# Pooled attention and a three-way max FFN on one core: long-run loads, pooling by adds on GpSimd, paired q transposes, 128-token value tiles and 512-token FFN blocks

## Chip, cores, metric

One core of one Trainium2 chip. The metric is the time of one execution on the device in microseconds (us), the median of several. "Span" is the time from the first to the last instruction in a profiled execution, some 2 to 3 us less. Outputs are compared with the reference.

Names: PE is TensorE (PEld its weight loads), DVE VectorE, ACT ScalarE, POOL GpSimd, SP the sync engine, which here only issues transfers. L189 is line 189 of the kernel in question; a trailing `q` (SPq, POOLq) is an engine's sequencer, where transfers are issued.

## The reference

```python
# q, k, v: [8 batches, 8 heads, 576 tokens, 64], float32
k_p = k.reshape(B, H, 72, 8, D).mean(axis=3)          # pooled over 8 tokens
v_p = v.reshape(B, H, 72, 8, D).mean(axis=3)
attn = softmax(q @ k_p.T / sqrt(64))                  # 576 x 72 for each head
x = (attn @ v_p) as [4608 tokens, 512]                # heads side by side
h = max(x @ w1, x @ w2, x @ w3)                       # w: [512, 768]
out = h @ w_out                                       # [768, 512], float32
```

## The kernel before

Tokens are kept in their order. For each batch: q is transposed, k and v are pooled by matmuls with a 0/1 matrix, then scores, exp, values, transposes; the FFN of batch b-1 fills TensorE beside batch b's attention. The order of instructions on each engine is fixed when the kernel is built.

```python
# q: runs of 2 tokens (512 B); one transpose for each of 36 [128 tokens, 64] pieces
qsrc = q[b]....rearrange("(g p j) d -> p g j d", p=128, j=2)
nc.gpsimd.dma_start(out=qb_, in_=qsrc)
for u in range(n_t):
    nc.tensor.transpose(pqt[:, u, :], qb_[:, tidx // 2, tidx % 2, :], ident)

# k, v: five loads each, runs of one token (256 B), pooled by 2 x 5 matmuls of 512 columns
for c in range(5):
    nc.gpsimd.dma_start(out=kvt, in_=src[b, :, CHUNK0[c]:CHUNK0[c] + 128, :]
                        .rearrange("h s d -> s h d"))
for c in range(5):
    nc.tensor.matmul(p, ptr[:, c, :], kvts[c], start=(c == 0), stop=(c == 4))

# values: 48 matmuls a batch with 96-wide weights
nc.tensor.matmul(pavn[:, 3 * i + j, :], eTs[i][:, QC * j:QC * j + QC], vp8[:, h, :], ...)

# FFN, for each batch: two halves of 288 columns, and five output tiles (the fifth half used)
for i in range(2):
    for jc in range(6):
        for wi in range(3):
            for kc in range(4):
                nc.tensor.matmul(pw, w_sb[wi][:, kc, ...], xT[:, kc, ncol], ...)
for m in range(5):
    n0, r0 = (128 * m, 0) if m < 4 else (448, 64)
    ...
# ... (cut)
```

The softmax here doesn't subtract the row's maximum and nothing guards it: scores larger than these inputs give would overflow.

Of the kernel before, what the change touches and what calls it, by code (L numbers as in the profile page):

```python
# [14 lines left out]
def kernel(  # L15
# [23 lines left out]
    HALF = 288  # L39
    QC = 96  # L40
    NG = (H * S) // 256
    KCH = C // 128
    JCH = DFF // 128

    const = ctx.enter_context(tc.tile_pool(name="const", bufs=1))
    wtsp = ctx.enter_context(tc.tile_pool(name="wts", bufs=1))
    sb1 = ctx.enter_context(tc.tile_pool(name="sb1", bufs=1))
    sb2 = ctx.enter_context(tc.tile_pool(name="sb2", bufs=2))
    sb3 = ctx.enter_context(tc.tile_pool(name="sb3", bufs=3))
    kvsb = ctx.enter_context(tc.tile_pool(name="kvsb", bufs=12))  # L50
    psp = ctx.enter_context(tc.tile_pool(name="psp", bufs=1, space=bass.MemoryType.PSUM))

    def q_load(b):
        qb_ = sb1.tile([128, NG, 2, D], BF16, name="qb", tag="qb")
        qsrc = q[b].rearrange("h s d -> (h s) d").rearrange(
            "(g p j) d -> p g j d", p=128, j=2)
        nc.gpsimd.dma_start(out=qb_, in_=qsrc)  # L57
        return qb_

    qb0 = q_load(0)  # L60
# [6 lines left out]
    CHUNK0 = [0, 128, 256, 384, 448]  # L67
    ptf = const.tile([128, 5, 128], F32, name="ptf", tag="ptf")
    nc.gpsimd.memset(ptf, 0.0)
    for c in range(5):  # L70
        o = CHUNK0[c]
        pz = ptf[:, c, 0:Sp]
        nc.gpsimd.memset(pz, 1.0)
        nc.gpsimd.affine_select(out=pz, in_=pz, compare_op=ALU.is_ge, fill=0.0,
                                base=o, pattern=[[-8, Sp]], channel_multiplier=1)
        nc.gpsimd.affine_select(out=pz, in_=pz, compare_op=ALU.is_ge, fill=0.0,
                                base=7 - o, pattern=[[8, Sp]],
                                channel_multiplier=-1)
        if c == 4:
            nc.gpsimd.affine_select(out=pz, in_=pz, compare_op=ALU.is_ge,  # L80
                                    fill=0.0, base=-64, pattern=[[0, Sp]],
                                    channel_multiplier=1)
    ptr = const.tile([128, 5, 128], F16, name="ptr", tag="ptr")
    nc.scalar.copy(out=ptr, in_=ptf)
    bias8 = const.tile([128, 1], F32, name="bias8", tag="bias8")
    nc.gpsimd.memset(bias8, float(POOL))

    w_sb = [wtsp.tile([128, KCH, DFF], F16, name=f"mw{wi}", tag=f"mw{wi}")
            for wi in range(3)]
    wo_sb = wtsp.tile([128, JCH, C], F16, name="mwo", tag="mwo")  # L90

    def load_weights():
        for t, wap in zip(w_sb, (moe_w1, moe_w2, moe_w3)):
            nc.gpsimd.dma_start(out=t,
                                in_=wap.rearrange("(kc p) j -> p kc j", p=128))
        nc.gpsimd.dma_start(out=wo_sb,
                            in_=moe_w_out.rearrange("(jc p) c -> p jc c", p=128))

    def preproc_q(b, qb_):
        qT = sb2.tile([128, NG * 256], BF16, name="qT", tag="qT")  # L100
        nc.gpsimd.memset(qT[64:128, :], 0.0)  # L101
        qTv = qT[0:64].rearrange("d (g p j) -> d g j p", p=128, j=2)
        for grp in range(5):
            n_t = 8 if grp < 4 else 4
            pqt = psp.tile([64, 8, 128], BF16, name="pqt", tag="misc", bufs=2)
            for u in range(n_t):
                tidx = grp * 8 + u
                nc.tensor.transpose(pqt[:, u, :], qb_[:, tidx // 2, tidx % 2, :],  # L108
                                    ident)
            g0 = grp * 4  # L110
            nc.scalar.copy(out=qTv[:, g0:g0 + n_t // 2, :, :], in_=pqt[:, 0:n_t, :])  # L111
        return qT

    def pool_kv(b):
        ps = {}
        for name, src in (("k", k), ("v", v)):
            p = psp.tile([128, H * D], F32, name=f"p{name}8", tag="misc", bufs=2)
            kvts = []
            for c in range(5):
                kvt = kvsb.tile([128, H, D], F16, name=f"{name}c", tag="kv")  # L120
                nc.gpsimd.dma_start(  # L121
                    out=kvt,
                    in_=src[b, :, CHUNK0[c]:CHUNK0[c] + 128, :].rearrange(
                        "h s d -> s h d"))
                kvts.append(kvt)
            for c in range(5):
                nc.tensor.matmul(p, ptr[:, c, :], kvts[c],  # L127
                                 start=(c == 0), stop=(c == 4))
            ps[name] = p
        kp8 = sb2.tile([Sp, H, D], BF16, name="kp8", tag="kp8")  # L130
        nc.scalar.copy(out=kp8, in_=ps["k"][0:Sp].rearrange("sp (h d) -> sp h d", d=D))
        pkt = psp.tile([64, H, Sp], BF16, name="pkt", tag="misc", bufs=2)
        for h in range(H):
            nc.tensor.transpose(pkt[:, h, :], kp8[:, h, :], ident[0:Sp, 0:Sp])
        kpT = sb2.tile([128, H, Sp], BF16, name="kpT", tag="kpT")
        nc.gpsimd.memset(kpT[64:128, :, :], 0.0)
        nc.scalar.copy(out=kpT[0:64], in_=pkt)
        vp8 = sb2.tile([Sp, H, 65], F16, name="vp8", tag="vp8")
        nc.scalar.copy(out=vp8[:, :, 0:D],
                       in_=ps["v"][0:Sp].rearrange("sp (h d) -> sp h d", d=D))  # L140
        nc.scalar.activation(out=vp8[:, :, D:65], in_=ps["v"][0:Sp, 0:H],
                             func=FT.Identity, bias=bias8[0:Sp], scale=0.0)
        return kpT, vp8

    def heads(b, qT, kpT, vp8, xnat):
        for h in range(H):
            pavn = psp.tile([QC, 2 * 3, 65], F32, name="pavn", tag="att", bufs=3)
            eTs = []
            for i in range(2):
                col0 = S * h + HALF * i  # L150
                psc = psp.tile([Sp, HALF], F32, name="psc", tag="att", bufs=3)
                nc.tensor.matmul(psc, kpT[:, h, :], qT[:, col0:col0 + HALF],  # L152
                                 start=True, stop=True)
                eT = sb3.tile([Sp, HALF], F16, name="eT", tag="eT")
                nc.scalar.activation(out=eT, in_=psc, func=FT.Exp,  # L155
                                     scale=1.0 / 64.0)
                eTs.append(eT)
            for i in range(2):
                for j in range(3):
                    nc.tensor.matmul(pavn[:, 3 * i + j, :],  # L160
                                     eTs[i][:, QC * j:QC * j + QC],
                                     vp8[:, h, :], start=True, stop=True)
            rcp = sb2.tile([QC, 6], F32, name="rcp", tag="rcp")
            nc.vector.reciprocal(out=rcp, in_=pavn[:, :, 64])  # L164
            nc.vector.tensor_tensor(  # L165
                out=xnat[:, :, D * h:D * h + D], in0=pavn[:, :, 0:D],
                in1=rcp.to_broadcast([QC, 6, D]), op=ALU.mult)

    def xpose(b, xnat, xT):
        for cj in range(6):  # L170
            pxt = psp.tile([128, KCH, QC], F16, name="pxt", tag="misc", bufs=2)
            for kc in range(KCH):
                nc.tensor.transpose(pxt[:, kc, :],  # L173
                                    xnat[:, cj, 128 * kc:128 * kc + 128],
                                    identh[0:QC, 0:QC])
            nc.scalar.copy(out=xT[:, :, QC * cj:QC * cj + QC], in_=pxt)  # L176

    def moe(b, xT):
        hT = sb2.tile([128, JCH, S], F16, name="hT", tag="hT")
        for i in range(2):  # L180
            ncol = bass.ts(i, HALF)
            for jc in range(JCH):
                t1 = t2 = None
                for wi in range(3):
                    tag, nb = ("m1a", 2) if wi != 1 else ("m1b", 1)
                    pw = psp.tile([128, HALF], F32, name=f"pw{wi}", tag=tag,
                                  bufs=nb)
                    for kc in range(KCH):
                        nc.tensor.matmul(  # L189
                            pw, w_sb[wi][:, kc, bass.ts(jc, 128)],  # L190
                            xT[:, kc, ncol],
                            start=(kc == 0), stop=(kc == KCH - 1))
                    if wi == 0:
                        t1 = sb2.tile([128, HALF], F32, name="t1", tag="t1")
                        nc.vector.tensor_copy(out=t1, in_=pw)  # L195
                    elif wi == 1:
# [18 lines left out]
    for b in range(B):  # L215
        qT = preproc_q(b, qb0 if b == 0 else q_load(b))
        kpT, vp8 = pool_kv(b)
        if b == 0:
            load_weights()
# [38 lines left out]
```

## Time and profile before

| | before |
|---|---|
| time | 346.65 us (346.37 to 346.81, three runs); 342.7 to 347.8 in later calls |
| span of the profiled run | 343.5 us |
| TensorE busy | 90% |
| software queue's share of the 16 DMA engines | 67.8% |

The lines of this profile, and how they are read, are in the prediction.

### The profile page before, as it was taken

How to read it: one execution, taken by the hardware profiler on the slowest of the kernel's cores; microseconds unless marked ns; L12 is line 12 of the kernel's file. 1: busy time of each engine (PE TensorE's matmuls, PEld its weight loads, DVE VectorE, ACT ScalarE, POOL GpSimd, SP SyncE). 2: the span in 40 equal slices, each digit the busy share in tenths (PEclk: the TensorE clock that was granted, in tenths of full speed). 3: DMA queues.
4: the chain of work that ended last, by engine and by line, in shares of the span. 5: the costliest groups of instructions: out<-in, count | busy, mean ns of one | idle time of the engine just before them, and what ended most of it. 6: DMA issues, size and time to landing. Idle time of an engine off the chain costs nothing.

```text
span 343.5 us, 6436 instructions
## 1 busy us (share of the span) xinstructions
PE 309.8 (90%) x2528; PEld 203.4 (59%) x2528; DVE 165.9 (48%) x416; ACT 151.7 (44%) x290; POOL 122.9 (36%) x134
## 2 busy tenths in 40 slices
PE   0678589999999999999999999999999999999992
PEld 0425366665567566675567556765577466766750
DVE  0004226771387326771387226761487227764840
ACT  1634364435753275505753276406743286412012
POOL 8997259650744029500743028500800000000000
PEclk9999999999999999999999999999999999999999
DMA  7999999943890219903990229903990210003012
GB/s 69 68 153 209 186 127 117 110 31 124 89 148 2 90 52 159 66 0 131 91 140 0 94 52 159 62 1 138 97 96 0 103 37 2 2 14 125 0 41 101
DMA packets 109408, 28.22 MB, mean 82 GB/s; under 512 B 102464, under 2 KB 104768, under 8 KB 109376
## 3 DMA queue, kind: packets, MB, share of 16 engines
q0 software_dynamic: 104128, 18.36, 67.8%
q1 hardware_dynamic: 5248, 9.44, 7.6%
q8 instruction: 20, 0.33, 0.4%
q14 instruction: 12, 0.10, 0.1%
HBM read 36.70 MB, written 9.44 MB: 134 GB/s over the span
## 4 chain that ended last, share of the span: by engine, by line
PE 68%; ACT 15%; DMA 8%; POOL 6%; issue 3%; ACTq 0%; DVE 0%; POOLq 0%
PE pw L189 33%; PE po L207 14%; ACT qT L111 9%; PE pavn L160 7%; DMA qb<-in_q_dram 6%; ACT eT L155 4%; PE psc L152 3%; PE pqt L108 3%; PE pxt L173 3%; PE pk L127 2%; PE pv L127 2%; DMA out_dram<-osb 2%; POOL vc L121 1%; POOL kc L121 1%; POOL qT L101 1%
## 5 line engine op out<-in xcount | busy, mean ns | idle before, releaser
L189 PE MATMUL pw<-xT,mw 128*128 128x288 f16 x1152 | 180.0, 287 | 0.2
L189 PEld LDWEIGHTS <-mw 128*128 128x128 f16 x1152 | 106.2, 99 | 25.3 <-issue 0.6
L195 DVE COPY t<-pw 128x288 f32<-128x288 f32 x96 | 43.5, 453 | 64.0 <-PE pw L189 62.5
L155 ACT ACTIVATE eT<-psc 72x288 f16<-72x288 f32 x128 | 46.5, 402 | 40.9 <-PE psc L152 39.8
L210 ACT COPY osb<-po 128x512 f32<-128x512 f32 (+1 forms) x40 | 23.4, 584 | 93.0 <-PE po L207 76.4
L201 DVE TENSOR_TENSOR hT<-t,pw 128x288 f16<-128x288 f32 x96 | 42.9, 447 | 36.6 <-PE pw L189 31.3
L207 PE MATMUL po<-mwo,hT 128*128 128x512 f16 x240 | 53.3, 379 | 1.5 <-ACT osb L210 1.5
L198 DVE TENSOR_TENSOR t<-t,pw 128x288 f32<-128x288 f32 x96 | 43.3, 451 | 23.3 <-PE pw L189 17.2
L111 ACT COPY qT<-pqt 64x1024 bf16<-64x1024 bf16 (+1 forms) x40 | 43.9, 1184 | 19.6 <-PE pqt L108 19.0
L160 PEld LDWEIGHTS <-eT 72*96 72x96 f16 x384 | 31.4, 130 | 28.6 <-ACT eT L155 24.6
L160 PE MATMUL pavn<-vp,eT 72*96 72x65 f16 x384 | 40.0, 220 | 5.8 <-ACT eT L155 2.0
L57 POOL DMA_DIRECT2D qb<-in_q_dram x8 | 9.9, 1234 | 95.3 <-PE pqt L108 72.9
L207 PEld LDWEIGHTS <-hT 128*128 128x128 f16 x240 | 23.5, 98 | 28.5 <-issue 1.8
L121 POOL DMA_DIRECT2D vc<-in_v_dram x40 | 35.3, 918 | 9.9 <-DMA mwo<-in_moe_w_out_dram 2.9
L108 PE MATMUL pqt<-ident,qb 128*64 128x128 bf16 x288 | 25.1, 236 | 14.8 <-DMA qb<-in_q_dram 11.7
L101 POOL MEMSET qT<- 64x4608 bf16 x8 | 31.6, 3946 | 18.7 <-PE psc L152 18.6
L121 POOL DMA_DIRECT2D kc<-in_k_dram x40 | 35.2, 898 | 2.5 <-PE psc L152 1.9
L165 DVE TENSOR_TENSOR xnat<-pavn,rcp 96x384 f16<-96x384 f32 x64 | 35.1, 548 | 0.8
L108 PEld LDWEIGHTS <-qb 128*64 128x64 bf16 x288 | 21.1, 120 | 23.4 <-DMA qb<-in_q_dram 12.3
L152 PE MATMUL psc<-qT,kpT 128*72 128x288 bf16 x128 | 34.8, 308 | 0.0
L164 DVE RECIPROCAL rcp<-pavn 96x6 f32<-96x6 f32 x64 | 12.2, 190 | 40.8 <-PE pavn L160 40.5
L176 ACT COPY xT<-pxt 128x384 f16<-128x384 f16 x48 | 20.8, 479 | 17.4 <-PE pxt L173 16.9
(31 smaller groups left out, 119.6 us busy)
## 6 DMA issues: line engine op xcount, KB each, us to landing
out_dram<-osb SPq DMA_DIRECT2D x32, 256.0 KB, 2.0
kc<-in_k_dram POOLq DMA_DIRECT2D x40, 128.0 KB, 6.6
vc<-in_v_dram POOLq DMA_DIRECT2D x40, 128.0 KB, 6.9
qb<-in_q_dram POOLq DMA_DIRECT2D x8, 576.0 KB, 7.1
mw<-in_moe_w_dram POOLq DMA_DIRECT2D x3, 768.0 KB, 12.3
out_dram<-osb SPq DMA_DIRECT2D x8, 128.0 KB, 2.3
mwo<-in_moe_w_out_dram POOLq DMA_DIRECT2D x1, 768.0 KB, 18.3
```

Source lines behind the costliest of these rows:

```text
L108: nc.tensor.transpose(pqt[:, u, :], qb_[:, tidx // 2, tidx % 2, :], ident)
L111: nc.scalar.copy(out=qTv[:, g0:g0 + n_t // 2, :, :], in_=pqt[:, 0:n_t, :])
L121: nc.gpsimd.dma_start(out=kvt, in_=src[b, :, CHUNK0[c]:CHUNK0[c] + 128, :].rearrange("h s d -> s h d"))
L152: nc.tensor.matmul(psc, kpT[:, h, :], qT[:, col0:col0 + HALF], start=True, stop=True)
L155: nc.scalar.activation(out=eT, in_=psc, func=FT.Exp, scale=1.0 / 64.0)
L160: nc.tensor.matmul(pavn[:, 3 * i + j, :], eTs[i][:, QC * j:QC * j + QC], vp8[:, h, :], start=True, stop=True)
L165: nc.vector.tensor_tensor(out=xnat[:, :, D * h:D * h + D], in0=pavn[:, :, 0:D], in1=rcp.to_broadcast([QC, 6, D]), op=ALU.mult)
L189: nc.tensor.matmul(pw, w_sb[wi][:, kc, bass.ts(jc, 128)], xT[:, kc, ncol], start=(kc == 0), stop=(kc == KCH - 1))
L195: nc.vector.tensor_copy(out=t1, in_=pw)
L198: nc.vector.tensor_tensor(out=t2, in0=t1, in1=pw, op=ALU.max)
L201: nc.vector.tensor_tensor(out=hT[:, jc, ncol], in0=t2, in1=pw, op=ALU.max)
L207: nc.tensor.matmul(po, hT[:, jc, n0:n0 + 128], wo_sb[:, jc, :], start=(jc == 0), stop=(jc == JCH - 1))
```

## The change

The intent: less work for TensorE (pooling by adds on an idle engine, fewer and fuller transposes, no half-used output tile) and loads in long runs. To let two q tokens of a partition be transposed at once, tokens are reordered inside the kernel: column 32 t + r of a batch is token 18 r + t, and the stores put them back, 32 rows at a time.

```diff
-        qsrc = ... "(g p j) d -> p g j d", p=128, j=2          # runs of 512 B
+        kt <- k[b] "(p i j d) -> p i j d", p=96, i=6, j=8      # SP's queue, 12288 B runs
+        vt <- v[b] "h (sp j) d -> sp h j d", j=8               # SP's queue, 2048 B runs
+        qb <- q[b] "(g p t d) -> p g t d", g=2, p=128, t=18    # POOL's queue, 4608 B runs
+    (two buffers each)
-                nc.tensor.matmul(p, ptr[:, c, :], kvts[c], ...)        # pooling, 10 a batch
+        eng = nc.vector if b == 0 else nc.gpsimd
+            for n in (4, 2):
+                e.tensor_tensor(out=t[:, :, 0:n, :], in0=t[:, :, 0:n, :],
+                                in1=t[:, :, n:2 * n, :], op=ALU.add)
+            for o in outs:
+                e.tensor_tensor(out=o, in0=t[:, :, 0, :], in1=t[:, :, 1, :], op=ALU.add)
+        fold(eng, kt, [kp2[:, :, 0, :], kp2[:, :, 1, :]])
+        fold(nc.gpsimd, vt, [vp_all[:, b, :, 0:D]])
-                nc.tensor.transpose(pqt[:, u, :], qb_[:, tidx // 2, tidx % 2, :], ident)
+                nc.tensor.transpose(pqt[:, u, :], qb[:, g, 2 * i:2 * i + 2, :], ident)
-                    nc.tensor.matmul(pavn[...], eTs[i][:, QC * j:QC * j + QC], vp8[:, h, :], ...)
+        for n in ((128, 128, 128, 128, 64) if b % 2 == 0 else (64, 128, 128, 128, 128)):
+                nc.tensor.matmul(pav[0:n, ...], ets[h][:, c0:c0 + n], vp_all[:, b, h, :], ...)
-    def moe(b, xT):      # 2 x 288 columns, 5 output tiles
+    def moe(n):          # 512 columns across batches, 4 output tiles
+                if wi == 0: nc.scalar.copy(out=t, in_=pw)       # the first copy goes to ScalarE
+            for u in range(4):
+                nc.sync.dma_start(out=dst[:, g, :], in_=osb[32 * u:32 * u + 32, :])
 ... (cut; PSUM is now: scores 2 banks, values 2 banks, transposes 1 bank, FFN 3 banks)
```

The four weight loads are issued by POOL straight after batch 0's q. xT holds all 4608 tokens.

## The prediction

> **What bounds the kernel now.** I read the page first: which engine is full, at which clock, and what the path to the end runs through.
>
> ```profile
> PE 309.8 (90%) x2528; PEld 203.4 (59%) x2528; DVE 165.9 (48%) x416; ACT 151.7 (44%) x290; POOL 122.9 (36%) x134
> ...
> PE   0678589999999999999999999999999999999992
> ...
> PEclk9999999999999999999999999999999999999999
> DMA  7999999943890219903990229903990210003012
> ...
> PE 68%; ACT 15%; DMA 8%; POOL 6%; issue 3%; ACTq 0%; DVE 0%; POOLq 0%
> ```
>
> TensorE is busy 90% of 343.5 us at full clock, no other engine over half. The first five slices (8.6 us each) are its only thin ones. So the time is TensorE work, plus a start, plus what is lost between. The DMA engines are full at the start only. The groups give mean durations, but matmuls overlap (1152 of 287 ns would be 331 us, busy is 180), so I take the step from one start to the next in the timeline:
>
> ```profile
> 298.80 7.27 PE L189 MATMUL pw<-xT,mw 128*128 128x288 f16 x58
> ...
> 305.91 6.64 PE L207 MATMUL po<-mwo,hT 128*128 128x512 f16 x30
> ```
>
> 58 steps in 7.11 us: 122.6 ns for 288 columns. In the chain the 30 po matmuls take 6.47 us: 215.7 ns for 512. The same way, from one batch's TensorE timeline:
>
> ```profile
> 159.09 0.63 PE L108 MATMUL pqt<-ident,qb 128*64 128x128 bf16 x8
> 159.66 1.28 PE L189 MATMUL pw<-xT,mw 128*128 128x288 f16 x9
> ...
> 165.47 1.24 PE L127 MATMUL pk<-kc,ptr 128*128 128x512 f16 x5
> 166.55 1.24 PE L127 MATMUL pv<-vc,ptr 128*128 128x512 f16 x5
> ...
> 182.25 0.33 PE L173 MATMUL pxt<-identh,xnat 96*128 96x96 f16 x4 [0.15 <-ACT xT L176]
> 182.41 0.29 PE L189 MATMUL pw<-xT,mw 128*128 128x288 f16 x1
> ```
>
> q transposes step 71 ns (0.57/8), pooling matmuls 216 ns, output transposes 40 ns (0.16/4); from their neighbours, scores 125 ns, values about 48 ns, k transposes 47 ns. Work of one batch: 144 x 122.6 + 30 x 215.7 = 24.1 us of FFN; 36 x 71 + 10 x 216 + 8 x 47 + 16 x 125 + 48 x 48 + 24 x 40 = 10.4 us of attention. Eight batches: 276 us. The po blocks start 38.3 us apart in the chain, so 3.8 us per batch is lost to short waits, mostly 0.15 to 0.25 us before a matmul that needs a ScalarE result. The remaining 67.5 us of the span: about 34 us in the start (dense FFN from 46 us, about 12 us of work done by then), 27 us in seven periods, 6.5 us in the tail (two output buffers waiting for the store).
>
> The start is not one wait:
>
> ```profile
> 8.26 1.92 PE L108 MATMUL pqt<-ident,qb 128*64 128x128 bf16 x16 [8.26 <-DMA qb<-in_q_dram]
> ...
> 44.07 1.92 PE L108 MATMUL pqt<-ident,qb 128*64 128x128 bf16 x16 [3.48 <-DMA qb<-in_q_dram]
> ```
>
> q lands at 8.3 us; then ten k/v loads and the weights are issued one by one by POOL, batch 0's attention crawls head by head, and the second q, queued behind the weights, holds TensorE until 44 us.
>
> **What the Trainium skill says.** (1) "TensorE: Matmul & The Clock Gate", section "Wait — 56ns, not 53.3ns?": a warm stream steps N/2.4 GHz plus about 2.5 ns. The trace agrees: 122.6 for 288, 215.7 for 512. So a longer matmul saves only the 2.5 ns. (2) Same page, "Weight-path perf modes": the fast weight load needs exactly 128 weight columns. The trace fits: 128-wide pxt steps 40 ns, just its 96 columns; 64-wide pqt steps 71 where its 128 columns are 53. (3) "GPSIMD Engine Reference", section 3: a two-input fp32 add of 2048 elements takes 4497 ns, 2.2 ns an element, about twice VectorE. No trace here has one. (4) "DMA: Bandwidth & Descriptors", Specifications: line rate needs runs of 512 B or more. The page has 102464 of 109408 packets under 512 B and the software queue at 67.8%, which agrees, but TensorE hardly waits for DMA after 46 us.
>
> **The change, part by part, on TensorE.**
> - FFN blocks of 512 tokens: 9 blocks x (72 + 24) x 215.7 ns = 186.4 us, against 8 x 24.1 = 193. Gain 6.6 us: 5.2 of it from the fifth, half-wasted output tile of each batch, only 1.4 from longer matmuls.
> - Pooling on POOL: removes 10 x 216 ns, 2.16 us a batch, **17 us** in all. POOL's adds: k 1536+768+2x384 and v 2048+1024+512 elements a partition, 6656 x 2.2 ns = an estimate of 14.6 us a batch from (3). That is half of a period and runs ahead: hidden, except at the start.
> - Paired q transposes: 18 instead of 36, each 128-wide, estimated at 56 ns: 1.0 us against 2.56, gain **12 us**.
> - Values: 40 instead of 48, 128-wide weights except the last tile, about 40 ns: 1.66 against 2.3 us, gain 5 us. k transposes 6 x 40 ns; output transposes 16 x 56 + 4 x 30 ns = 1.0 us; scores stay at 2.0 us. All nearly nothing.
> Attention becomes 1.0 + 0.24 + 2.0 + 1.66 + 1.0 = 5.9 us a batch, 47 us in all. **TensorE work: 186.4 + 47.2 = 233.6 us, 42 us less.**
>
> Other engines, by the trace's slopes (ScalarE 384 columns 479 ns, 512 columns 585; VectorE 288 columns 450 ns, 384 columns 548): ScalarE gets the first FFN copy: 10 x 0.585 a block; per batch three q copies at 0.80, eight exps of 576 at 0.64, five xT copies at 0.585, 10.4 us. Sum 9 x 5.85 + 8 x 10.4 = 136 us. VectorE: 12 x 0.68 a block, 5.9 us a batch: 121 us. Neither becomes a bound.
>
> **What is lost around it.** Start: k and v go out by the sync queue, q and the weights by POOL at once. Weights and second q took about 18 us for 7.4 MB read in the old trace, so some 400 GB/s; k, v, q of batch 0, the weights and batch 1's loads are 13.4 MB, 34 us. q and k of batch 0 at about 9 us; q transposes in one PSUM buffer until 14.5; k transposes and two VectorE copies until 17; eight heads, one score buffer, 1.35 us each, until 28; v's adds on POOL end near 24; four value tiles at 1.9 us and the copy: FFN from about 37 us, up to 46 if TensorE's fixed order has the second q's transposes (landing near 35 us) ahead of the values. About 7 us of work is done by then: I choose a loss of **33 us**, hardly better than before. Steady: about 21 waits a batch (8 scores, 5 values, 5 output transposes, 4 others; before some 20 that cost anything) with single score, value and transpose buffers, but FFN matmuls to fill; I choose 3 us x 7 = **21 us**. Tail: four stores a tile at 0.33 us issue, 2 us landing, three output buffers: **5 us**. Span 233.6 + 33 + 21 + 5 = 292.6; the time is 3.1 us over the span now, so 296; since xT holds all tokens, attention can run ahead and the last two blocks or so should be free of waits, which I put at 4 us: **292 us**.
>
> **Rivals.**
> 1. *The single buffers become the bound* (two-bank scores, two-bank values, one transpose bank). The serial chain of a batch is about 8 x 1.2 + 5 x 1.9 + 3 x 1.5 + 2.5 = 26 us against 29 us of TensorE work per batch (233.6/8): close. For it: the order within each engine is fixed, and now the first FFN copy sits in ScalarE's line behind exps. Against it: FFN work depends on none of these buffers, and parts of successive batches overlap. It would give 310 to 320 us.
> 2. *The start gets worse or POOL's adds hold it*: POOL has q, four weights and v's adds in one queue, and the weights take half the bandwidth from k and v. For it: the old trace shows just such a wait for q. Against it: no ten loads one after another. Worth 10 us more: 302.
> 3. *Nearly all is packed*: waits below 1.5 us a batch, FFN from 33 us: 275 us.
> 4. *The transfers were the bound*: the long runs would then be the gain. TensorE's 90% and the DMA row's zeros in mid-kernel speak against it; I give this part nothing after the start.
>
> **Range and chances.** Work is known to within a few us, the start to 8 either way, steady loss to 10, a common cause (a poor order) only upwards: 276 to 312. For less than 2% gain (over 339.7 us) the 42 us would have to be lost almost wholly again, for which only rival 1 at its worst has room: faster 0.96, within 2% 0.03, slower 0.01.
>
> **What would show it.** Right: 864 FFN matmuls (1392 before), stepping 215.7 ns in dense stretches; pqt stepping near 56 ns, values near 40; no pk or pv; POOL adds near 2.2 ns an element with no long wait on them after batch 1; DMA packets down to a tenth; ScalarE near 136 and VectorE near 121 us busy; first pw between 33 and 46 us. Wrong: TensorE waits on exps, VectorE's normalisation or transposes of over 5 us a batch (rival 1), on POOL's adds or q in the first 60 us (rival 2), or small matmuls that do not step as narrow columns suggest, which would raise the 47 us.

## The result, and the profile after

| | time, median | runs | ratio to before, 95% interval |
|---|---|---|---|
| before | 346.51 us | 342.74 to 346.81 | |
| after | 307.96 us | 306.41 to 308.39 | 0.891, 0.886 to 0.896 |

A ratio is the mean time of one kernel's fast runs over the mean of the other's of the same rounds, so it is not quite the ratio of the two medians. The kernel before had medians of 346.5, 345.7, 345.2 and 345.6 us in the four calls, so times of different calls compare to about 1 us.

The page of the kernel after:

```profile
PE 257.3 (84%) x1664; PEld 130.4 (43%) x1664; DVE 127.8 (42%) x211; ACT 133.0 (43%) x219; POOL 124.6 (41%) x72
...
PE   0144470299999999999999999999999999999991
...
PEclk9999996579999999999999999999999999999998
DMA  7999999988644986982610450050022003104014
```

TensorE is less busy than before and the thin start is longer: eight slices of 7.7 us, the seventh empty. Behind it the row is full. The same in stretches (columns: busy us of each engine with the number of instructions, the granted TensorE clock, the DMA engines' busy share, GB/s):

```profile
0.00:41.25 41.25, 13.40 (x97) 9.04 (x97) 13.50 (x18) 11.19 (x16) 25.38 (x23) 1.00 0.99 234
41.25:45.20 3.95, 3.94 (x12) 1.07 (x11) 0.82 (x2) 0.86 (x2) 3.93 (x3) 1.00 1.05 263
45.20:59.58 14.38, 0.00 (x0) 0.00 (x0) 0.69 (x1) 0.00 (x0) 14.12 (x7) 0.61 0.96 227
59.58:258.73 199.15, 198.56 (x1365) 101.65 (x1366) 96.30 (x167) 108.71 (x180) 81.15 (x41) 0.99 0.43 99
```

The FFN begins at 41 us, does eight matmuls, and then TensorE stands still for 14.4 us with the DMA engines full. What it waits for, in the timeline and among the issues (columns: queue, count, KB each, median us from issue to landing):

```profile
18.97 4.49 POOL L98 TENSOR_TENSOR vt<-vt 72x2048 f32<-72x2048 f32 x1 [12.91 <-DMA vt<-in_v_dram]
...
23.41 0.74 POOL L64 DMA_DIRECT2D qb<-in_q_dram  x1
...
59.59 0.82 PE L114 MATMUL pqt<-ident,qb 128*128 128x128 bf16 x6 [14.40 <-DMA qb<-in_q_dram]
60.20 1.91 PE L179 MATMUL pw<-xT,mw 128*128 128x512 f16 x4
61.91 0.85 PE L114 MATMUL pqt<-ident,qb 128*128 128x128 bf16 x6
```

```profile
qb<-in_q_dram POOLq DMA_DIRECT2D x8, 576.0 KB, 8.6
mw<-in_moe_w_dram POOLq DMA_DIRECT2D x3, 768.0 KB, 27.5
mwo<-in_moe_w_out_dram POOLq DMA_DIRECT2D x1, 768.0 KB, 50.8
```

Batch 1's q is issued by POOL at 23.4 us, behind v's first add, and lands 36.1 us later; the last weight load, issued at 5.2 us, takes 50.8 us. Meanwhile SP has fetched k and v ahead: its issues are at 0.7, 1.2, 1.7, 2.1, 12.4, 31.1, 41.2, 45.5 and 52.7 us.

The wait has a second cost. The four FFN matmuls behind it take 1.71 us to the next start, 427 ns each instead of the 216 of later stretches; by the starts in the trace this lasts until 65.4 us. The granted clock of this stretch is 0.59 (third figure from the right):

```profile
59.58:66.70 7.12, 7.11 (x38) 4.06 (x39) 1.07 (x2) 2.98 (x4) 1.27 (x2) 0.59 0.80 197
```

Steps of 426 ns also follow the waits of 7.1 us in q1_first and 12.2 us in kv_single, and none follow one of 3.5 us in combined (216 ns).

The work itself steps as forecast. From the chain and the TensorE timeline of the kernel after:

```profile
258.73 15.54 PE pw L179 x72
274.27 5.18 PE po L196 x24
```

```profile
162.14 0.42 PE L151 MATMUL pav<-vp,et 72*128 72x65 f16 x8
162.40 1.89 PE L179 MATMUL pw<-xT,mw 128*128 128x512 f16 x8
...
172.55 0.50 PE L114 MATMUL pqt<-ident,qb 128*128 128x128 bf16 x6
172.89 1.03 PE L179 MATMUL pw<-xT,mw 128*128 128x512 f16 x4
```

15.54/72 and 5.18/24 are 215.8 ns; the paired transposes step 0.34/6 = 57 ns, the 128-wide values 0.26/8 = 33 ns. The account takes the forecast's steps for all three columns; with the steps as measured the work after is some 231 us, and the loss between some 17:

| us | before | predicted | after |
|---|---|---|---|
| TensorE's work | 276 | 233.6 | 233.6 |
| lost in the start | 34 | 33 | 52 (59.6 less 7.6 of work done) |
| lost between | 27 | 17 (21 less 4) | 14.5 (199.15 less 184.6) |
| lost at the end | 6.5 | 5 | 6.4 (300.2 to 306.6) |
| time over span | 3.1 | 3.1 | 1.8 |

### The profile page after: what moved, and what is told of

Read it like the earlier page. It is cut to its first block, busy times and chain, and to the rows that moved or that the text cites. A ratio compares the mean times of both kernels' runs of the same rounds, so it can differ in the third digit from the quotient of the medians.

```text
span 306.6 us, 4320 instructions
## 1 busy us (share of the span) xinstructions
PE 257.3 (84%) x1664; PEld 130.4 (43%) x1664; DVE 127.8 (42%) x211; ACT 133.0 (43%) x219; POOL 124.6 (41%) x72
## 2 busy tenths in 40 slices
DMA packets 17078, 36.47 MB, mean 119 GB/s; under 512 B 2720, under 2 KB 5024, under 8 KB 16288
## 3 DMA queue, kind: packets, MB, share of 16 engines
q1 hardware_dynamic: 12512, 28.32, 35.7%
## 4 chain that ended last, share of the span: by engine, by line
PE 78%; DMA 18%; POOL 1%; DVE 0%; ACT 0%; issue 0%; SPq 0%; ACTq 0%
PE pw L179 46%; PE po L196 15%; DMA qb<-in_q_dram 12%; DMA vt<-in_v_dram 6%; PE psc L135 5%; PE pav L151 4%; PE pqt L114 3%; PE pxt L164 3%; POOL vt L98 1%; PE pkt L120 1%; DVE t L187 0%; DVE xn L159 0%; ACT xT L168 0%; ACT osb L200 0%; SPq L58 0%
## 5 line engine op out<-in xcount | busy, mean ns | idle before, releaser
L179 PE MATMUL pw<-xT,mw 128*128 128x512 f16 x648 | 162.0, 386 | 0.1
L179 PEld LDWEIGHTS <-mw 128*128 128x128 f16 x648 | 57.8, 99 | 53.9 <-issue 2.5
L187 DVE TENSOR_TENSOR t<-t,pw 128x512 f16<-128x512 f16 x54 | 37.0, 686 | 88.9 <-PE pw L179 77.7
L98 POOL TENSOR_TENSOR vt<-vt 72x2048 f32<-72x2048 f32 (+1 forms) x16 | 54.8, 3425 | 16.1 <-DMA vt<-in_v_dram 15.6
L138 ACT ACTIVATE et<-psc 72x576 f16<-72x576 f32 x64 | 41.4, 646 | 34.1 <-PE psc L135 34.1
L190 DVE TENSOR_TENSOR hT<-t,pw 128x512 f16<-128x512 f16 x54 | 37.0, 685 | 29.9 <-PE pw L179 28.5
L184 ACT CAST t<-pw 128x512 f16<-128x512 f32 x54 | 31.6, 585 | 41.1 <-PE pw L179 40.4
L98 POOL TENSOR_TENSOR kt<-kt 96x1536 f32<-96x1536 f32 (+1 forms) x14 | 36.6, 2614 | 3.1 <-DMA kt<-in_k_dram 2.7
L135 PE MATMUL psc<-qT,kz 128*72 128x288 bf16 x128 | 29.5, 304 | 6.3 <-ACT et L138 5.1
L200 ACT COPY osb<-po 128x512 f32<-128x512 f32 x36 | 21.1, 587 | 16.7 <-PE po L196 15.1
L159 DVE TENSOR_TENSOR xn<-pav,rcp 128x512 f16<-128x512 f32 (+1 forms) x40 | 27.5, 687 | 1.0
L114 PEld LDWEIGHTS <-qb 128*128 128x128 bf16 x144 | 11.4, 109 | 38.3 <-DMA qb<-in_q_dram 29.5
L64 POOL DMA_DIRECT2D qb<-in_q_dram x8 | 6.0, 752 | 33.7 <-PE pqt L114 32.9
## 6 DMA issues: line engine op xcount, KB each, us to landing
kt<-in_k_dram SPq DMA_DIRECT2D x8, 1152.0 KB, 12.4
mwo<-in_moe_w_out_dram POOLq DMA_DIRECT2D x1, 768.0 KB, 50.8
```

What stands on the lines that cost most here:

```text
L98: e.tensor_tensor(out=t[:, :, 0:n, :], in0=t[:, :, 0:n, :], in1=t[:, :, n:2 * n, :], op=ALU.add)
L114: nc.tensor.transpose(pqt[:, u, :], qb[:, g, 2 * i:2 * i + 2, :], ident)
L135: nc.tensor.matmul(psc[:, par, 0:288], kz[:, par, h, :], mov, start=True, stop=True)
L138: nc.scalar.activation(out=et.rearrange("p (i a r) -> p i a r", a=2, r=NR), in_=psc[:, :, 0:288].rearrange("p a (i r) -> p i a r", r=NR), ...
L159: nc.vector.tensor_tensor(out=xn[0:n], in0=pv[:, :, :, 0:D], in1=rcp[0:n].to_broadcast([n, 2, 4, D]), op=ALU.mult)
L179: nc.tensor.matmul(pw, w_sb[wi][:, kc, bass.ts(jc, 128)], xT[:, kc, col], start=(kc == 0), stop=(kc == KCH - 1))
```

## The experiments

All are edits of the kernel after. First the start. Theory A: the wait is one of place in the software queue. Rival B: it is the bytes, whatever the order. Theory C: early fetches of k and v take the bandwidth.

### q1_first

```diff
     first = load(0)
+    q1 = q_load(1)                      # before the four weight loads
```

> Batch 1's q is issued right after batch 0's, ahead of the four weight loads; nothing else changes. Theory A (place in the software queue: q of batch 1 waits behind v's adds on POOL and behind the weights): it lands near 20 us, the 14.4 us wait of TensorE before it is gone, time 292 to 297 us. Rival B (it is the bytes: 19 MB must come in before TensorE can go on, whatever the order): the wait moves to the weights or to k and v, time over 303 us.

Measured: 302.24 us (301.29 to 304.14), ratio 0.874. Between the two expectations. The wait for q is gone: TensorE runs from 43.4 to 77.8 us without a gap. But then it stands still again. Stretches, then one line of the waits and one of the stores:

```profile
43.37:77.80 34.43, 34.38 (x226) 17.04 (x226) 14.90 (x27) 17.58 (x29) 33.86 (x18) 1.00 0.94 223
77.80:87.00 9.20, 2.10 (x17) 1.23 (x15) 1.15 (x2) 1.29 (x2) 9.04 (x4) 0.74 0.57 149
```

```profile
ACT osb L206 <- DMA out_dram<-osb: 9.1, 4, 7.6
```

```profile
DMA to landing us min/median/max: 1.6/1.7/13.7
```

ScalarE waited 7.6 us for an output buffer (first line), and TensorE for ScalarE. The second line is of the stores (L210): the first four were issued from 70.5 to 71.9 us and landed only at 84.6 to 85.0, up to 13.7 us later; a k load that SP had issued at 68.3 us landed at 84.2. Later stores also waited up to 6.8 us in SP's line, but the wait of ScalarE ended with the first four. So A is right about the first wait: q lands at 21.5 us and the 14.4 us are gone. Of these some 9 came back: 7.1 us of idle TensorE in this stretch, on a wait that the first one had covered, and 2.1 us because the FFN began at 43.4 instead of 41.3 us.

### kv_single

```diff
-        kt = ld.tile([96, 6, POOL, D], F32, name="kt", tag="kt")
+        kt = ld.tile([96, 6, POOL, D], F32, name="kt", tag="kt", bufs=1)      # vt likewise
```

> One buffer each for k and v instead of two, so k and v of later batches can't be fetched until the adds have read the earlier ones; q stays behind the weights. Theory A alone: q of batch 1 still waits behind 6.3 MB of weights, time within 3 us of 308. Theory C (the early fetches of k and v of batches 1 to 4 take the weights' and q's bandwidth): q of batch 0 lands near 9 us instead of 14.3, q of batch 1 near 40 instead of 59.6, time 288 to 297 us. If the single buffers hold POOL's adds back later, a wait on k or v of some us per batch shows after 60 us.

Measured: 307.66 us (306.94 to 308.22), the same as the kernel after. Yet C's mechanism is there: the last weight load lands after 29.2 us instead of 50.8, batch 1's q lands at 38.3 us instead of 59.5, and its transposes start at 44.4 us without any wait for q. (Batch 0's q lands at 13.3 us, not near 9: the early fetches delay it by only 1 us.) C's forecast of the time fell all the same, since a wait of the same size came later:

```profile
ACT osb L200 <- DMA out_dram<-osb: 13.6, 3, 12.5
```

With one buffer, SP has to hold each k and v load until POOL's adds have read the one before (40.4 us of waiting for the adds of v in SP's line), and the stores stand behind it in the same line: the first is issued at 81.2 us.

### q1_first_kv_single

Both edits.

> Both edits. If A and C both hold and add: first FFN matmul near 36 us, no wait for q after it, time 284 to 290 us. If one makes the other needless: equal to the better of the two alone, within 2 us.

Measured: 306.82 us (306.05 to 307.97). Neither expectation: it is like kv_single, worse than q1_first alone. The two don't add; the single buffers cost what q's place saved.

### q1_first_kv_pool

```diff
     def load(b, qb=None):
+        eng = nc.sync if b == 0 else nc.gpsimd
-        nc.sync.dma_start(out=kt, ...)          # vt likewise
+        eng.dma_start(out=kt, ...)
```

> On top of q1_first: k and v of batches 1 to 7 are issued by POOL (software queue) behind the weights instead of by SP, so SP's queue carries only batch 0's loads and the stores. Theory D (in q1_first the 14.4 us of the first wait were saved at 45 us, but 9 us came back near 78 us since the first stores stand behind k and v loads in SP's line): the output wait there is gone and the whole of the saving shows, time 287 to 294 us. Rival (POOL's adds, 15.3 us a batch from 19 us on, are what holds TensorE in the first 90 us): the wait moves to POOL's results, time 299 to 305 us.

Measured: of four runs two were fast, 296.94 and 298.70 us, and two counted as slow (302.85, 310.36); ratio of the fast ones 0.864. Faster than q1_first by 4 to 5 us, but between the two expectations: slower than theory D's 287 to 294, and just below the rival's 299 to 305. The two count as slow only because they are over 1.5% above the fastest; a spread of 13 us in four runs is wide, and its cause is open. The profile fell on the slow run at 310.36 us, so its remaining waits are only a hint: near 139 us ScalarE waits 4.4 us for an output buffer, and the slowest store of that run takes 10.0 us to land. In combined, too, with the loads in POOL's queue, one takes 8.5 us, against a median of 1.7. So a store can be slow with the loads in another queue, and theory D's line at SP is not shown to be the cause of the slow stores.

### q1_first_stores_act

```diff
-                nc.sync.dma_start(out=dst[:, g, :], in_=osb[32 * u:32 * u + 32, :])
+                nc.scalar.dma_start(out=dst[:, g, :], in_=osb[32 * u:32 * u + 32, :])
```

> On top of q1_first: the 144 stores are issued by ScalarE's queue instead of SP's, loads stay as they are. Theory D as before: the stores no longer stand behind loads in one line, no 9 us wait near 78 us, less what 144 issues of some 0.35 us cost ScalarE (50 us more of its time, on the path only where TensorE waits for it): time 292 to 300 us. If the stores were slow because the engines were full of k and v: still 7 us or more of waiting for a store, time over 300 us.

Measured: 335.0 us (332.86 to 336.78). By its letter the second branch (over 300 us, long waits for stores), but 35 us beyond it. Stores land slowly from this queue as well, up to 8.4 us against 13.7 in q1_first, and a second kind of wait is there: ScalarE is the engine that frees the FFN's PSUM buffers, and while it stands at a store everything behind it stands. Its waits in that profile: 45.4 us for stores to free output buffers, 15.1 the longest; VectorE waited 83.4 us for ScalarE's first FFN copies. Its DMA row shows the engines at nine tenths from 8 to 75 us, so how much of this is slow stores and how much is ScalarE's line being the wrong place for them can't be told apart by this run.

Now the parts of the change, each undone by itself.

### pool_matmuls_back

```diff
+        if b >= 2:
+            for kv in range(2):
+                pd = psp.tile([128, C], F32, name="pd", tag="pw", bufs=3)
+                for c in range(5):
+                    nc.tensor.matmul(pd, identh, wo_sb[:, c, :], start=(c == 0), stop=(c == 4))
```

> The ten 512-column pooling matmuls of a batch put back as dead work (two groups of five into an FFN buffer that nobody reads, the result stays right), in batches 2 to 7. The prediction's term is 10 x 216 ns a batch: six batches 13 us, time 319 to 322 us if TensorE's work is what counts after the start. If part of it falls into TensorE's waits: 310 to 316 us.

Measured: 321.56 us (320.95 to 322.77), 13.6 us more, against 13.0 expected. After the start TensorE's work counts in full, and the pooling term of 17 us for eight batches stands.

### few_adds

```diff
-            for n in (4, 2):
+            for n in ():                # wrong result on purpose: tokens 0 and 1 only
```

> Wrong result on purpose: k and v are pooled by one add instead of three, which leaves POOL about a quarter of its adding. If POOL's adds are hidden, as predicted, except at the start: q of batch 1 is issued some 8 us earlier, time 300 to 308 us, and after the first FFN block the same course. If they pace the batches (rival 2): 295 us or less, with shorter rounds after 90 us.

Measured: 308.68 us (306.90 to 310.23), the same as the kernel after; the result is wrong, as meant. POOL is busy 33.7 us instead of 124.6. The page and one line of the timeline:

```profile
PE 257.0 (84%) x1664; PEld 130.1 (42%) x1664; DVE 125.2 (41%) x209; ACT 133.1 (43%) x219; POOL 33.7 (11%) x42
```

```profile
59.41 0.82 PE L114 MATMUL pqt<-ident,qb 128*128 128x128 bf16 x6 [10.50 <-DMA qb<-in_q_dram]
```

From these transposes to the end both kernels take 247.0 us, so 91 us of POOL's adding cost nothing after the start. In the start the run changes more than the adds: k's and v's buffers come free earlier, SP fetches earlier (k of batch 2 at 9.7 us instead of 12.4), batch 0's q lands at 17.9 us instead of 14.3 and the FFN begins at 44.9 instead of 41.3; the wait for q covers that. And q, issued at 20.2 us instead of 23.4, lands at the same 59.4 us: when POOL gets round to issuing it did not decide here.

### q_single_transposes

```diff
-                nc.tensor.transpose(pqt[:, u, :], qb[:, g, 2 * i:2 * i + 2, :], ident)
+                for par in range(2):
+                    nc.tensor.transpose(pqt[64 * par:64 * par + 64, u, :],
+                                        qb[:, g, 2 * i + par, :], ident)
```

> The changed kernel with each token of a pair transposed by itself: 36 transposes a batch with 64-wide weights instead of 18 with 128-wide; same layout, same copies. The prediction's term is 36 x 71 against 18 x 56 ns, 1.55 us a batch, 12 us in all: time 318 to 322 us if each step takes 71 ns and is on the path. If neighbours that fill different halves of the columns overlap, or the steps hide beside waits: 308 to 313 us.

Measured: 310.08 us (309.48 to 312.54), ratio 0.901 with an interval of 0.895 to 0.907 that overlaps the one of the kernel after: at most a few us. The timeline says why:

```profile
146.00 0.53 PE L115 MATMUL pqt<-ident,qb 128*64 128x128 bf16 x12
146.46 1.04 PE L180 MATMUL pw<-xT,mw 128*128 128x512 f16 x4
```

Twelve 64-wide transposes take 0.46 us up to the next matmul, 38 ns each, less than the 53 ns that their 128 columns alone take at the rate of the longer matmuls. The single starts in the trace (the view merges them) say more: the two of a pair start 3 or 4 ns apart and the pairs step some 56 ns, so two transposes in different halves run at once; after the last one it is 152 ns to the FFN's matmul. In the kernel before, where all filled the same column half, the transposes stepped 55 or 56 ns too, and it was 151 ns from the last of a group to the FFN's matmul: the 71 ns of the prediction is a mean over a group of eight with its pauses, and not a step. The Trainium skill, "TensorE: Matmul & The Clock Gate", Part 3 (packing small matmuls), says that matmuls in different column groups of the array run at the same time, and alternate halves do just that here. The 12 us between old and new transposes are real as a difference of the two traces, but by this run most of them would have been had with single transposes in alternate halves: 36 x 38 = 1.37 us a batch against 1.0, an estimated 3 us in all, where the times differ by 2.1.

### ffn_per_batch

```diff
-    NB = 512
+    NB = 288                            # two halves a batch, as before
-        for mm in range(4):
+      for mm in range(5):
+            n0, r0 = (128 * mm, 0) if mm < 4 else (448, 64)
```

> The changed kernel with the old FFN blocking put back: per batch two halves of 288 columns and five output tiles, the fifth half used. The prediction's term: 8 x 24.1 against 9 x 20.7 us of TensorE, 6.6 us more: time 312 to 317 us. If VectorE and ScalarE fixed costs (192 instead of 108 maxima) hold TensorE too: over 318 us. If the blocks' gain was only in the waits: under 310 us.

Measured: 324.25 us (323.74 to 324.94), 16.3 us more: the upper branch. The work term is 6.6. The chain shows rounds of 33.4 and 32.7 us where the work is 24.1 + 5.9 = 30.0:

```profile
185.57 6.47 PE po L198 x30
...
218.98 6.47 PE po L198 x30
...
251.70 6.47 PE po L198 x30
```

So 2.7 to 3.4 us a round are lost, against 1.6 on average in the kernel after once its clock is full (six rounds in 169.3 us from 89.4 to 258.7 us, for 26.6 us of work each): about 10 us in seven rounds, which with the work makes the 16. With 288 columns VectorE has 192 maxima and ScalarE 96 copies instead of 108 and 54 (453 and 400 ns each); that this is what lengthens the pauses fits, but no run isolates it.

### small_tile_last

In the timeline of the kernel after, head rounds took 1.16 us in even batches and 1.36 us in odd ones, which begin with the 64-token tile. Theory E: its 64-wide weights cost that.

```diff
-        for n in ((128, 128, 128, 128, 64) if b % 2 == 0
-                  else (64, 128, 128, 128, 128)):
+        for n in (128, 128, 128, 128, 64):
```

> Every batch ends with its 64-token value tile; in the changed kernel the odd batches begin with it. Theory E (seen in the trace: in odd batches each head's first value matmul, with 64-wide weights between score and FFN matmuls, costs TensorE some 0.2 us, 1.36 us a head against 1.16): four batches x eight heads x 0.2 us = 6.4 us less, time 300 to 303 us. Rival (the longer round comes from the batch's place against the FFN blocks, not from the tile's width): within 1.5 us of 308.

Measured: 301.57 us (300.92 to 302.60), 6.4 us less, as forecast. Two head rounds of the kernel after, then two of this one, in the TensorE timeline:

```profile
124.32 0.41 PE L135 MATMUL psc<-qT,kz 128*72 128x288 bf16 x2
124.66 0.22 PE L151 MATMUL pav<-vp,et 72*64 72x65 f16 x1
124.81 1.04 PE L179 MATMUL pw<-xT,mw 128*128 128x512 f16 x4
125.68 0.41 PE L135 MATMUL psc<-qT,kz 128*72 128x288 bf16 x2
```

```profile
124.15 0.41 PE L135 MATMUL psc<-qT,kz 128*72 128x288 bf16 x2
124.40 0.20 PE L150 MATMUL pav<-vp,et 72*128 72x65 f16 x1
124.43 1.03 PE L178 MATMUL pw<-xT,mw 128*128 128x512 f16 x4
125.29 0.41 PE L135 MATMUL psc<-qT,kz 128*72 128x288 bf16 x2
```

The 64-wide matmul starts 0.34 us after the scores instead of 0.25, and the FFN matmul behind it 0.15 us later instead of 0.03: some 0.2 us for one matmul of 65 columns. The change pays this 32 times. It is not the 64-wide matmul as such: where eight follow each other they step 33 ns, like the 128-wide. The extra time is at the change: 215 ns instead of 122 from the second score matmul to it, and 150 instead of 33 from it to the FFN's. The transposes of the kernel before show the same at the end of each group (151 instead of 56 ns).

### kv_short_runs

```diff
-        nc.sync.dma_start(out=kt, in_=ksrc)
+        for par in range(2):                               # even and odd tokens: 256 B runs
+            nc.sync.dma_start(out=kt[:, :, par::2, :], in_=ksrc[:, :, par::2, :])
+        for h in range(H):
+            for par in range(2):
+                nc.sync.dma_start(out=vt[:, h, par::2, :], in_=vsrc[:, h, par::2, :])
```

> k and v come in runs of 256 B as in the old kernel (k as two transfers, v as sixteen, even and odd tokens apart), into the same layout. If long runs matter only at the start (the prediction gave them nothing later): DMA packets back to some 90000, q of batch 1 lands 5 to 20 us later than 59.6, time 312 to 328 us, and after that the same course. If they matter in the steady part too: waits on k or v after 70 us and over 330 us. If they don't matter: within 2 us of 308.

Measured: 344.89 us (344.50 to 345.86): the whole gain is gone. The prediction gave long runs nothing after the start, and that fell. But not by way of the DMA engines: SP's queue takes 36.0% of them against 35.7%, with 82432 packets instead of 12512. It is the issuing: SPq holds 18% of the chain that ended last, and 0% in the kernel after. First the kernel after, then this one (duration of an issue in ns, least, median, most):

```profile
L61 SPq DMA_DIRECT2D vt<-in_v_dram x8: 306/374/455, 1.2 to 125.3; - x8
```

```profile
L66 SPq DMA_DIRECT2D vt<-in_v_dram x128: 790/791/13058, 3.5 to 273.7; - x128
```

A batch's sixteen v issues take 12.6 us of SP's line and two k issues 2.6; batch 0's sixteen take 37.0 us, with the DMA row at nine tenths, so there full engines may be behind it. The stores stand in that line too; POOL waits up to 28.5 us for v. The number of transfers went up with the shorter runs, so this run does not price the run length alone, and it says nothing about the software queue that the kernel before used. That price stays open.

### combined

q1_first, k and v by POOL, the small tile last, and one more edit:

```diff
-            osb = sb3.tile([128, C], F32, name="osb", tag="osb")
+            osb = sb3.tile([128, C], F32, name="osb", tag="osb", bufs=8)
```

> q of batch 1 first, k and v of batches 1 to 7 issued by POOL, the small tile last, and eight output buffers instead of three (with k and v on POOL's queue the first stores landed late, up to 10 us, and TensorE waited for an output buffer). If the causes add: 308 less 11 (q1_first_kv_pool's fast runs) less 6 less 3: 286 to 290 us. If the slow stores still hold it: 293 to 298 us.

Measured: 289.64 us (288.69 to 290.60, six runs), ratio to the kernel before 0.839 (0.835 to 0.843): 18.3 us faster than the change, and the causes add. The stretches:

```profile
0.00:41.30 41.30, 13.63 (x97) 9.11 (x98) 13.70 (x19) 11.20 (x16) 17.27 (x20) 1.00 0.99 208
41.30:100.00 58.70, 54.35 (x387) 28.08 (x385) 28.44 (x49) 30.27 (x50) 42.85 (x24) 1.00 0.58 129
100.00:240.00 140.00, 139.76 (x997) 73.38 (x995) 69.22 (x120) 80.33 (x133) 73.64 (x44) 1.00 0.54 126
```

From 41 us on TensorE is idle 4.4 us up to 100 us and 0.2 us in the next 140. Most of the 4.4 is a wait for POOL, which the longer wait for q had covered in the kernel after:

```profile
PE pkt L127 <- POOL kp L108: 3.5, 1, 3.5
```

Idle time is not all that is lost, though: by the same count the kernel after lacks only 0.6 of its 199 us, and its steps say some 17. By the steps, combined loses some 36 us before its FFN begins at 41.1 us, some 14 from there to 239 us (these 4.4, 1.4 to the lower clock, the rest in short pauses) and 7 at the end. So the start is the largest part left. The share of the eight output buffers by themselves was not run.

## Why the prediction was right, and where it was not

The class and the range held (276 to 312 us), at the upper edge: 292 against 308.

- **TensorE's work** came out as worked, 231 for 233.6 us: 864 FFN matmuls at 215.8 ns, transposes at 57 ns; the values at 33 ns instead of 40, 2.7 us in all. Pooling is confirmed by its undoing (13.6 for 13.0 us). The FFN term of 6.6 us was too small: undone it cost 16.3, the work and about 10 us of pauses. The transposes' 12 us are right as the difference of the two kernels, but the reason was misread: 64-wide transposes do not step 71 ns for want of a fast weight load, they step 56, and the rest is one pause in each of a batch's five groups (k transposes the same: 33 ns and a pause, not 47). Half as many steps give some 8 us, the pauses that went the rest. No run undoes the values' 5 us.
- **The start was the mis-sized term**: 33 us predicted, 52 measured: 19 us, more than the whole miss of 16. The step that failed is "TensorE's fixed order has the second q's transposes (landing near 35 us) ahead of the values", with its 46 us as the worst case. They stood behind the values and eight FFN matmuls, and q landed only at 59.5 us. I had divided 13.4 MB by 400 GB/s, and both numbers were wrong. SP's queue went on to fetch k and v of batches 2 and 3 and k of batch 4 as soon as buffers came free, in the same engines while q waited: by 59.5 us the trace has 9.2 MB landed by SP's queue and 4.7 by POOL's, as 16-bit values of twice that size in memory, so 18.6 MB read at 313 GB/s. At 400 GB/s that would be 46.5 us, so about half of the 24.5 us is the bytes and half the rate (an estimate from these figures). Also batch 0's q landed at 14.3 us instead of 9, so the FFN could begin at 41 and not at 37; why so late is open. kv_single shows the fetches' part (q at 38 us, last weight after 29 instead of 51 us), q1_first the order's (q at 21.5 us).
- **Lost between**: 17 predicted, 14.5 measured by the forecast's own steps, and that they agree is mostly luck. By the starts in the trace and the measured steps the loss is 16.8 us: 7.3 around the 64-wide value tile (6.4 came back in small_tile_last), 2.9 by the lower clock after the wait for q, and 6.7 in pauses, mostly under 0.2 us, where one kind of matmul follows another. I foresaw neither of the first two; the short waits that I had put at 17 us came to 6.7.
- **Rivals.** Rival 1 (single score, value and transpose buffers) did not happen: 14.5 us are lost in the 199 us after the start by the forecast's steps, and its 310 to 320 us would have needed 35 or more. Rival 2 was the right direction, by its q half and not by POOL's adds, which few_adds shows to be hidden after the start; I gave it 10 us and it was 19. (With q's wait gone, in combined, POOL's adds do hold TensorE for some 4 us.) Rival 4 (transfers) I dismissed after the start; kv_short_runs shows that the issue line of the loads can undo the whole gain.
- Tail 6.4 for 5, time over span 1.8 for 3.1, ScalarE 133 for 136 and VectorE 128 for 121 us busy (memsets and batch 0's adds, which I left out, are 8 of it): near enough. DMA packets fell to a sixth (17078 of 109408) and not to a tenth. The 3.1 us over the span compares a median with one profiled run; in the later calls the kernel before, too, is some 1.8 us over its span.

## What to carry to other kernels

When a kernel is bound by one engine, count its steps in the timeline: that part of a forecast held to about 1%. Take a step inside a run of equal matmuls, and price the change to another kind by itself: a mean over a group hid that here. Size the start by everything that is allowed to be in flight before the transfer that is waited for, prefetches of later rounds included, and by the order in each queue; then ask which wait comes next, since a removed wait of 14 us gave back only 6 while first stores took up to 13.7 us to land beside the loads. Order small odd pieces so that they don't come between large matmuls.

## What the Trainium skill lacked or had wrong

- "DMA: Bandwidth & Descriptors", section "Issuing engines are not separate DMA queues", says that transfers of all queues share the 16 engines and interleave. The runs agree, but neither that section nor the page's account of how an engine takes turns between queues gives a figure for what a deep prefetch on one queue does to another: here batch 1's q took 36.1 us to land behind the weights with k and v fetched ahead, and the last weight load 50.8 us, 29.2 with the fetches held back (kv_single).
- The same page has no figure for how the issue on SP grows when a transfer has many short runs: 0.79 us for a 72 KB load in 288 runs of 256 B, 13 us at worst, against 0.37 us for 1152 KB in 576 runs of 2048 B (kv_short_runs).
- "TensorE: Matmul & The Clock Gate", "Weight-path perf modes", has the condition of 128 columns, but not what narrower weights cost between others: some 0.2 us for one 64-wide value matmul, 6.4 us in all (small_tile_last), and nothing inside a run of 64-wide ones (33 ns a value). "TensorEngine Tiling (Array Packing)", "Key Properties", has a drain at a change of tiling mode, without a figure; whether that is what happens here was not shown.
- "TensorE: Matmul & The Clock Gate", Part 3, measures 32-wide pieces on 512 columns; 64-wide transposes in alternate halves are not there: 38 ns each with the change at the group's end, against 71 ns in the same half, counted alike.
- The same page, Part 4, gives a 128x128 bf16 transpose as about 275 ns in a kernel, its latency. In a stream it steps 57 ns here, and that is the figure that a sum of work needs.
- "GPSIMD Engine Reference", section 3, was right: 4504 ns for the 2048-element add, for its 4497.
